# Filler products taken out, first products reordered and last copies split in a convolution-and-MLP kernel

## The chip, the cores and the metric

The kernel runs on one core of a Trainium2 chip. A core has five engines that run side by side and meet only through semaphores: TensorE for matrix products (PE in the profile; PEld is its weight load, which may overlap the product before), VectorE (DVE), ScalarE (ACT), GpSimd (POOL) and SyncE (SP), which here only issues DMAs. Products land in PSUM, which the kernel cuts into tiles of two banks (128 partitions x 1024 floats). The metric is the device time of one execution in microseconds (us). The median of three runs of the kernel before is 217.84 us (217.82 to 217.86).

## The reference

For a sequence of 2048 tokens and 512 channels the layer computes, in bfloat16 in and out:

```python
k_shift = sum over t of k_pad[:, t:t+S, :] * shift_k[:, ks-1-t]      # 4 taps
kv   = k_shift * v
kv_f = rfft2(pad(kv, S), axes=(1, 2))      # length 4096
kf_f = rfft2(pad(ssm_k, S), axes=(1, 2))
y    = irfft2(kv_f * kf_f)[:S] + kv * ssm_D
h    = x + layernorm(x) * y
h2   = h + relu(layernorm(h) @ w1) @ w2
```

The middle axis has length one, so the transform is a one-dimensional convolution of `kv` with `ssm_k` along the tokens, done by a Fourier transform of length 4096.

## The kernel before, in words

The transform is written as two stages of matrix products in each direction. "K" is the filter `ssm_k` and "X" is `kv`; their stage-1 results are the tiles BK and BX in SBUF.

Before the transform, `fill` (L153) multiplies a tile of zeros 22 times while the first data arrive. `to_rows` (L270) turns a 128 x 2048 array into rows: four steps `h` of eight TensorE transposes into a PSUM tile `pst`, each copied out in one piece, by ScalarE for h = 0 and 2 (L278) and by VectorE for h = 1 and 3 (L280). For K the target is `kfl`, for X it is `xfl`. `stage1` (L283) then runs for eight groups `gb` for each of K and X. A group takes two PSUM tiles, `pss[0]` and `pss[1]`, 32 small products (L293), and copies out. For K, VectorE adds a mask `dmask` to one half of each tile (L305) while ScalarE copies the other half (L308). For X, ScalarE copies the first tile (L266) and VectorE the second (L268); in X's group 3 ScalarE copies both. With `more=1`, which all of X's groups have, a group begins with one product of zeros into `pss[1]` (L288, recorded at L156).

`taps` (L332) computes 512 tokens by two channel blocks of the shifted `k` with eight products (L336), and VectorE multiplies the result by `v` in place (L330). K's groups 0 to 5 alternate with `taps`; the last two `taps` stand ahead of K's group 6. X's `to_rows` can only start after the last of these products with `v`. K's group 7 comes behind X's transposes, then X's eight groups, then four products of zeros (L394).

The product stage (L436) makes 16 groups of three units: `sums` for two frequencies (L427), and `pairs` (L418) twice. Each unit multiplies tables by BK into the left half of a PSUM tile and by BX into the right half; ScalarE copies the left half out (L409) and VectorE multiplies it by the right half, back into BX or BK (L433). The tables of `sums`, `smc`, are built by GpSimd (L381).

Inverse stage 1 (`inv1`, L518) makes 16 steps `b`. A step takes one PSUM tile, four groups of three products (one from BX at L523, two from BK at L526), and two copies out, one for each parity `rho`, into `ax[0]` (in BX's memory) and `ax[1]`. One letter for each copy says which engine does it: both on ScalarE, both on VectorE, and in the last step one each. Four products of zeros follow (L557), then inverse stage 2 (`inv2`, L604), which needs all of `ax`, and the MLP in four chunks (L616, L629).

What sets the order: the kernel is scheduled by hand, so each engine runs its instructions in the order of the program text. Up to the end of inverse stage 1 all PSUM tiles come from one pool of four buffers in rotation (L93), so a fifth tile waits until the first has been read. The framework adds the semaphore waits. Early on, GpSimd fills constants, scales the table `r2` (L228), builds `dmask` (L230, L237); VectorE reduces `r2` with `wrap13` (L220, called at L318) and derives small per-row constants (L311 to L315) ahead of K's `to_rows`.

Of the kernel before, what the change touches and what calls it, by code (L numbers as in the profile page):

```python
# [56 lines left out]
def kernel(  # L57
# [170 lines left out]
    nc.gpsimd.tensor_scalar(out=r2, in0=r2, scalar1=n2c[:], scalar2=2048.0, op0=ALU.mult, op1=ALU.add)  # L228
    dmask = early.tile([P, 2, 2, 16, 2, DC], BF16, name="dmask")
    nc.gpsimd.memset(dmask[:], 0.0)  # L230
    for dp in range(2):
        row = slice(64 * dp, 64 * dp + 1)
        for rp in range(2):
            for sp in range(2):
                src = draw[row, 256 * rp:256 * rp + 256].rearrange("p (r u s l d) -> p r u s l d", r=2, s=2, l=2, d=2)[:, :, :, sp, :, dp]
                for w in range(2):
                    nc.gpsimd.tensor_copy(out=dmask[row, rp, sp, :, w].rearrange("p u (r l) -> p r u l", l=2), in_=src)  # L237


    k1o = consts.tile([P, 1], F32, name="k1o")  # L240
# [29 lines left out]
    def to_rows(src, h, fl):  # L270

        pst = bank2("pst").rearrange("p b (i c) -> p (b i) c", i=4)
        srcw = src.bitcast(F32).rearrange("p c (a w) -> p (c a) w", w=32)
        for i in range(8):
            nc.tensor.transpose(out=pst[:, i, :], in_=srcw[:, :, 8 * h + i], identity=identw[:])  # L275
        o = fl.bitcast(I32)[:, :, 8 * h:8 * h + 8]
        if h % 2 == 0:
            nc.scalar.copy(out=o.bitcast(F32), in_=pst.rearrange("p i c -> p c i"))  # L278
        else:
            nc.vector.tensor_single_scalar(out=o, in_=pst.bitcast(I32).rearrange("p i c -> p c i"),  # L280
                                           scalar=0, op=ALU.bitwise_or)

    def stage1(fl, B, gb, dmul=None, xe="AD", more=0):  # L283

        j, sp = gb // 2, gb % 2
        pss = [bank2("ps1").rearrange("p b (a w r l x) -> p (b a) (w r) l x", a=2, w=2, r=2, l=2) for _ in range(2)]
        if more:
            fill(pss[1].rearrange("p u c l x -> p (u c l x)")[:, 0:512], more)  # L288
        for gi in range(8):
            g = 16 * j + 4 * (gi // 2) + 2 * sp + gi % 2  # L290
            for f, first in ((f1hi, True), (f1lo, False)):
                for rp, rows in enumerate(halves):
                    nc.tensor.matmul(out=pss[rp][:, gi // 2, :, gi % 2, :],  # L293
                                     lhsT=fl[rows, 2 * g:2 * g + 2, :].rearrange("p d n -> p (d n)"),
                                     rhs=f[rows].rearrange("p w r v h -> p (w r v h)"), start=first, stop=not first,
                                     tile_position=(64 * rp, 0), skip_group_check=True)
        o = [B.rearrange("p i (u w) (v s) x -> p i u w v s x", w=2, s=2)[:, :, 4 * j:4 * j + 4, :, :, sp, 4 * rp:4 * rp + 4]
             .rearrange("p i u w v x -> p i (u w) v x") for rp in range(2)]
        pv = [p.rearrange("p u (w r) l (v i) -> p i (u w) v (r l)", w=2, i=2) for p in pss]
        if dmul is None:  # L300
            for rp in range(2):
                copy(xe[rp], o[rp], pv[rp])
            return
        for rp in range(2):
            nc.vector.tensor_tensor(out=o[rp][:, 0], in0=pv[rp][:, 0],  # L305
                                    in1=dmul[:, rp, sp, 4 * j:4 * j + 4].rearrange("p u w x -> p (u w) x").unsqueeze(2)
                                    .to_broadcast([P, 8, 16, 4]), op=ALU.add)
            nc.scalar.copy(out=o[1 - rp][:, 1], in_=pv[1 - rp][:, 1])  # L308

    for t, sh, op in ((0, 2, ALU.logical_shift_right), (1, 3, ALU.bitwise_and)):  # L310
        nc.vector.tensor_single_scalar(out=pi4[:, t:t + 1], in_=pi4[:, t:t + 1], scalar=sh, op=op)  # L311
    nc.vector.tensor_scalar(out=k1o[:], in0=pi4[:, 0:1], scalar1=2.0, scalar2=1.0, op0=ALU.mult, op1=ALU.add)
    nc.vector.tensor_copy(out=rof[:], in_=pi4[:, 1:2])
    for t, v in ((esc, TURN / 8192), (ebi, -0.5 * TURN)):
        nc.vector.tensor_scalar(out=t[:], in0=rows4[:], scalar1=rof[:], scalar2=v, op0=ALU.is_equal, op1=ALU.mult)  # L315
    for h in range(4):
        to_rows(sk, h, kfl)
    wrap13(r2)  # L318
    big_sin(st[:, :, 0:64], tsn, 1)

    def more_sines(i):
# [3 lines left out]
        else:  # L325
            big_sin(st[:, half, 64:128], r2[:, half], 1)

    def product(c, h, src):
        vv = vT[:, 2 * h:2 * h + 2, CH * c:CH * c + CH]
        nc.vector.tensor_tensor(out=vv, in0=src, in1=vv, op=ALU.mult)  # L330
# [13 lines left out]
    for gb in range(7):  # L344
        if gb == 6:
            taps(3, 0)
            taps(3, 1)
            ec_sins(0, (2, 3))
        stage1(kfl, BK, gb, dmask)
        if gb < 4:  # L350
            more_sines(gb)
        if gb == 1:
            ec_turns(0)
        if gb == 3:
            ec_wrap(0)
        if gb in (4, 5):
            ec_sins(0, (gb - 4,))
        if gb < 6:
            taps(gb // 2, gb % 2)
# [52 lines left out]
    def pairs(k1):  # L412

        ps = bank2("u")
        for x, B in enumerate((BK, BX)):
            for i, t in ((0, st[:, k1, 64:192]), (1, st[:, k1, 0:128])):
                for dp, pq in enumerate(halves):
                    nc.tensor.matmul(out=ps[:, dp, 256 * x:256 * x + 256], lhsT=t[pq], rhs=cols(B, pq, k1, i),  # L418
                                     start=(i == 0), stop=(i == 1), tile_position=(64 * dp, 0), skip_group_check=True)
        return ps[:, :, 256:512], forms(ps[:, :, 0:256], "ktu"), BK[:, :, :, k1, :]  # L420

    def sums(k1):
        ps = bank2("us")
        for k in (k1, k1 + 1):
            for x, B in enumerate((BK, BX)):
                for i in range(2):
                    nc.tensor.matmul(out=ps[:, k % 2, 256 * x:256 * x + 256], lhsT=smc[:, k // 4 % 4, i, k % 4, :],  # L427
                                     rhs=cols(B, slice(0, P), k, i), start=(i == 0), stop=(i == 1), skip_group_check=True)
        return ps[:, :, 256:512], forms(ps[:, :, 0:256], "kts"), BX[:, 0, :, k1:k1 + 2, :].rearrange("p g k x -> p k g x")

    def times(unit):
        ps, kt, o = unit
        nc.vector.tensor_tensor(out=o, in0=ps.rearrange("p b (g x) -> p b g x", x=8),  # L433
                                in1=kt[:].rearrange("p b (g x) -> p b g x", x=8), op=ALU.mult)
# [82 lines left out]

    def inv1(b, eng):  # L518
        ps = bank2("psi").rearrange("p b (i d a n) -> p (b i) d a n", i=2, d=2, a=2)
        for i in range(4):  # L520
            g = 4 * b + i
            o = ps[:, i].rearrange("p d a n -> p (d a n)")
            nc.tensor.matmul(out=o, lhsT=BX[:, 0, g // 2, :, g % 2::2].rearrange("p c r -> p (c r)"), rhs=inv3[:].rearrange("p d a n -> p (d a n)"),  # L523
                             start=True, stop=False, skip_group_check=True)
            for dp in range(2):
                nc.tensor.matmul(out=o, lhsT=BK[:, dp, g // 2, :, g % 2::2].rearrange("p c r -> p (c r)"),  # L526
                                 rhs=inv12[:, 2 - 2 * dp:6 - 2 * dp, :].rearrange("p a n -> p (a n)"),
                                 start=False, stop=(dp == 1), skip_group_check=True)
        for rho in range(2):
            copy(eng[rho], ax[rho][:, :, :, 8 * b:8 * b + 8],  # L530
                 ps.rearrange("p i d a n -> p a n (i d)")[:, rho].rearrange("p (n m) c -> p n m c", m=2))

    lift(0)
    column_means((0,))
# [179 lines left out]
```

## Time and profile before

| | before |
|---|---|
| median of 3 runs | 217.84 us |
| the profiled execution | 217.85 us |
| its span in the trace | 215.9 us |
| PE busy | 204.9 us, 95% of the span |
| DVE busy | 142.0 us, 66% |
| ACT busy | 114.8 us, 53% |
| POOL busy | 61.5 us, 28% |

The difference between the profiled execution and its span, 1.95 us, lies around the recorded instructions. "Busy" of PE counts a product from its start to a modelled end, and counts products of zeros as well. In the rows of the timeline a line reads: start, duration, engine, line of the kernel, operation, tile written <- tile read, shape, count, and in brackets how long the engine had been idle and what ended that. The chain of waits follows the end of the execution back through whatever released each instruction; its rows read: start, duration, engine, tile, line.

### The profile page before, as it was taken

The numbers are of one execution on the slowest core, as the hardware profiler recorded it, in microseconds if no ns is written. First come the engines' busy times: TensorE is split into PE (matmuls) and PEld (weight loads), VectorE is DVE, ScalarE is ACT, GpSimd is POOL, SyncE is SP. The second block draws the span as 40 slices with busy tenths as digits, with TensorE's granted clock in tenths as the row PEclk, the third lists the DMA queues.
The fourth block names the chain that finished last, engine by engine and source line by source line (L and its number), as shares of the span: only waits on it lengthen the run. The fifth ranks groups of instructions, "written<-read, shape, count | busy, mean of one in ns | idle before, by whom it ended". The sixth has DMA issues, their size and how long they took to land.

```text
span 215.9 us, 4338 instructions
## 1 busy us (share of the span) xinstructions
PE 204.9 (95%) x1750; PEld 138.8 (64%) x1750; DVE 142.0 (66%) x240; ACT 114.8 (53%) x183; POOL 61.5 (28%) x116
## 2 busy tenths in 40 slices
PE   7879999999999999999999999999999999999990
PEld 2465555876888888889998964448444844444440
DVE  6998988768487887789673296799068833261121
ACT  6677786688667767735586029700980056026300
POOL 7497505993365500032001102620202020002000
PEclk9999999999999999999999999999999999999998
DMA  5999960000700000035503996977916615010011
GB/s 164 329 221 187 190 93 3 0 5 6 258 3 0 3 0 3 0 97 100 97 3 98 277 204 125 216 141 130 125 22 121 137 33 100 25 53 20 0 53 47
DMA packets 47687, 19.93 MB, mean 92 GB/s; under 512 B 42706, under 2 KB 46132, under 8 KB 47668
## 3 DMA queue, kind: packets, MB, share of 16 engines
q1 hardware_dynamic: 44144, 16.15, 38.0%
q10 hardware_dynamic: 3524, 3.51, 5.6%
q8 instruction: 14, 0.23, 0.4%
q14 instruction: 5, 0.04, 0.1%
HBM read 7.02 MB, written 2.10 MB: 42 GB/s over the span
## 4 chain that ended last, share of the span: by engine, by line
PE 80%; DVE 11%; ACT 4%; issue 1%; DMA 1%; DVEq 0%
PE ps2m L629 18%; PE ps1m L616 14%; PE u L418 9%; PE us L427 9%; PE psi L526 7%; PE pkv L336 7%; PE ps L293 6%; PE pz L604 5%; PE psi L523 4%; PE pst L275 2%; ACT BX L261 2%; DVE E L44 1%; ACT BX L266 1%; DVE st L473 1%; ACT M L618 1%
## 5 line engine op out<-in xcount | busy, mean ns | idle before, releaser
L618 ACT ACTIVATE M<-ps1m 128x512 bf16<-128x512 f32 (+1 forms) x44 | 25.0, 602 | 49.8 <-PE ps1m L616 27.2
L629 PE MATMUL ps2m<-M 128*128 128x512 bf16 (+1 forms) x176 | 38.7, 379 | 0.0
L629 PEld LDWEIGHTS <-M 128*128 128x128 bf16 (+1 forms) x176 | 17.1, 98 | 20.9 <-ACT M L618 0.4
L616 PEld LDWEIGHTS <-w 128*128 128x128 bf16 (+1 forms) x176 | 17.4, 100 | 20.4 <-issue 0.8
L381 POOL TENSOR_TENSOR smc<-st 64x256 fp32r<-64x256 f32 x32 | 22.7, 728 | 13.2 <-PE us L427 12.3
L632 DVE SCALAR_TENSOR_TENSOR M<-ps2m,rstd,M 128x512 bf16<-128x512 f32 x12 | 9.0, 748 | 24.7 <-PE ps2m L629 16.2
L526 PE MATMUL psi<-inv,BK 128*128 128x256 f32 x128 | 23.2, 283 | 0.2 <-DVE BK L433 0.2
L477 POOL TENSOR_SCALAR rstd<-mv 128x4 f32<-128x4 f32 x8 | 2.2, 276 | 69.5 <-DVE mv L475 69.5
L433 DVE TENSOR_TENSOR BK<-u,ktu 128x512 fp32r<-128x512 f32 x32 | 20.4, 680 | 0.0
L526 PEld LDWEIGHTS psi<-inv,BK 128*128 128x128 f32 x128 | 20.2, 195 | 0.4 <-DVE BK L433 0.4
L616 PE MATMUL ps1m<-xT,w 128*128 128x512 bf16 (+1 forms) x88 | 19.6, 379 | 0.2 <-ACT M L618 0.2
L616 PE MATMUL ps1m<-M,w 128*128 128x512 bf16 (+1 forms) x88 | 19.3, 379 | 0.0
L523 PE MATMUL psi<-inv,BX 128*128 128x256 f32 x64 | 18.3, 286 | 0.0
L409 ACT COPY ktu<-u 128x512 f32<-128x512 f32 x32 | 17.2, 588 | 1.6
L433 DVE TENSOR_TENSOR BX<-us,kts 128x512 fp32r<-128x512 f32 x16 | 11.1, 692 | 9.0 <-PE u L418 9.0
L427 PE MATMUL us<-BK,smc 128*128 128x256 f32 x64 | 14.7, 311 | 0.0
L409 ACT COPY kts<-us 128x512 f32<-128x512 f32 x16 | 9.4, 588 | 9.9 <-PE us L427 9.9
L418 PE MATMUL u<-BK,st 64*128 64x256 f32 x128 | 14.6, 306 | 0.0
L427 PE MATMUL us<-BX,smc 128*128 128x256 f32 x64 | 13.1, 285 | 0.2 <-DVE BX L268 0.2
L308 ACT CAST BK<-ps 128x512 fp32r<-128x512 f32 x16 | 9.4, 586 | 7.1 <-PE ps L293 5.2
L418 PE MATMUL u<-BX,st 64*128 64x256 f32 x128 | 13.0, 282 | 0.0
L523 PEld LDWEIGHTS psi<-inv,BX 128*128 128x128 f32 x64 | 12.5, 195 | 0.3 <-DVE BK L433 0.2
(124 smaller groups left out, 399.7 us busy)
## 6 DMA issues: line engine op xcount, KB each, us to landing
E<-in_A_ssm_k_dram SPq DMA_DIRECT2D x1, 2048.0 KB
out_dram<-M ACTq DMA_DIRECT2D x16, 128.0 KB
w<-in_B_w_dram SPq DMA_DIRECT2D x1, 1376.0 KB
M<-in_B_w_dram ACTq DMA_DIRECT2D x1, 1280.0 KB
M<-in_A_q_dram SPq DMA_DIRECT2D x8, 128.0 KB
xh<-in_A_q_dram SPq DMA_DIRECT2D x4, 128.0 KB
xr<-in_A_q_dram SPq DMA_DIRECT2D x4, 128.0 KB
M<-in_B_w_dram ACTq DMA_DIRECT2D x1, 96.0 KB
```

Source lines behind the costliest of these rows:

```text
L293: nc.tensor.matmul(out=pss[rp][:, gi // 2, :, gi % 2, :], lhsT=fl[rows, 2 * g:2 * g + 2, :].rearrange("p d n -> p (d n)"), rhs=f[rows].rea ...
L336: nc.tensor.matmul(out=ps[:, i, :], lhsT=wdiag[:, 2 * h + i, j, :], rhs=kT[c][:, 2 * h + i, 16 - j:CH + 16 - j], start=(j == 0), stop=(j = ...
L381: nc.gpsimd.tensor_tensor(out=smc[pq, c % 4, i, :, 64 * dp:64 * dp + 64], in0=st[pq, ks, 64:128].bitcast(F32), in1=st[pq, ks, 0:64].bitcas ...
L409: nc.scalar.copy(out=kt[:], in_=ps)
L418: nc.tensor.matmul(out=ps[:, dp, 256 * x:256 * x + 256], lhsT=t[pq], rhs=cols(B, pq, k1, i), start=(i == 0), stop=(i == 1), tile_position= ...
L427: nc.tensor.matmul(out=ps[:, k % 2, 256 * x:256 * x + 256], lhsT=smc[:, k // 4 % 4, i, k % 4, :], rhs=cols(B, slice(0, P), k, i), start=(i ...
L433: nc.vector.tensor_tensor(out=o, in0=ps.rearrange("p b (g x) -> p b g x", x=8), in1=kt[:].rearrange("p b (g x) -> p b g x", x=8), op=ALU.mult)
L523: nc.tensor.matmul(out=o, lhsT=BX[:, 0, g // 2, :, g % 2::2].rearrange("p c r -> p (c r)"), rhs=inv3[:].rearrange("p d a n -> p (d a n)"), ...
L526: nc.tensor.matmul(out=o, lhsT=BK[:, dp, g // 2, :, g % 2::2].rearrange("p c r -> p (c r)"), rhs=inv12[:, 2 - 2 * dp:6 - 2 * dp, :].rearra ...
L616: nc.tensor.matmul(out=ps1[:fsz, :].rearrange("p (i t) -> p i t", i=4), lhsT=w1[:, c, fc * P:fc * P + fsz], rhs=hT[sc][:, :, c, :], start= ...
L618: nc.scalar.activation(out=h1T[:fsz, fc, :], in_=ps1[:fsz, :], func=ACT.Relu)
L629: nc.tensor.matmul(out=ps2[:], lhsT=h1T[:ksz, fc, i * P:(i + 1) * P], rhs=w2[:ksz, fc, :], start=(fc == 0), stop=(fc == NFC - 1))
```

## The change

Nine edits, in the order of the program:

- GpSimd scales `r2` behind the construction of `dmask` and not ahead of it.
- In `to_rows`, step h = 3 is copied out in two pieces, the first bank by ScalarE and the second by VectorE. This holds for K and for X.
- VectorE does K's `to_rows` copies first, then `wrap13(r2)`, then the small constants.
- `taps(3, 1)` is multiplied by `v` in two instructions of 512 columns, one for each bank.
- X's groups of `stage1` have no product of zeros, and the four after them are gone.
- X's group 3 is shared by ScalarE and VectorE as the other groups are.
- In the product stage, `sums` puts K's four products ahead of X's four. In the first group (k1 = 0) K's products of all three units come ahead of X's products of all three. The copies out (`forms`) are written behind the products.
- In `inv1`, step 0 issues the BX product of i = 0 and of i = 2 first. In step 15 ScalarE copies both parities of the first bank (i = 0, 1) and VectorE both parities of the second (i = 2, 3), in pieces of 256 elements.
- Two products of zeros and not four follow inverse stage 1.

```diff
-    nc.gpsimd.tensor_scalar(out=r2, in0=r2, scalar1=n2c[:], scalar2=2048.0, op0=ALU.mult, op1=ALU.add)
     dmask = early.tile([P, 2, 2, 16, 2, DC], BF16, name="dmask")
...
+    nc.gpsimd.tensor_scalar(out=r2, in0=r2, scalar1=n2c[:], scalar2=2048.0, op0=ALU.mult, op1=ALU.add)
...
-        o = fl.bitcast(I32)[:, :, 8 * h:8 * h + 8]
-        if h % 2 == 0:
-            nc.scalar.copy(out=o.bitcast(F32), in_=pst.rearrange("p i c -> p c i"))
-        else:
-            nc.vector.tensor_single_scalar(out=o, in_=pst.bitcast(I32).rearrange("p i c -> p c i"),
-                                           scalar=0, op=ALU.bitwise_or)
+        o = fl.bitcast(I32)
+        for eng, i0, n in {0: (("A", 0, 8),), 1: (("D", 0, 8),), 2: (("A", 0, 8),), 3: (("A", 0, 4), ("D", 4, 4))}[h]:
+            oi, pi = o[:, :, 8 * h + i0:8 * h + i0 + n], pst[:, i0:i0 + n, :]
+            if eng == "A":
+                nc.scalar.copy(out=oi.bitcast(F32), in_=pi.rearrange("p i c -> p c i"))
+            else:
+                nc.vector.tensor_single_scalar(out=oi, in_=pi.bitcast(I32).rearrange("p i c -> p c i"),
+                                               scalar=0, op=ALU.bitwise_or)
...
-    def stage1(fl, B, gb, dmul=None, xe="AD", more=0):
+    def stage1(fl, B, gb, dmul=None):
...
-        if more:
-            fill(pss[1].rearrange("p u c l x -> p (u c l x)")[:, 0:512], more)
...
-                copy(xe[rp], o[rp], pv[rp])
+                copy("AD"[rp], o[rp], pv[rp])
...
+    for h in range(4):
+        to_rows(sk, h, kfl)
+    wrap13(r2)
     for t, sh, op in ((0, 2, ALU.logical_shift_right), (1, 3, ALU.bitwise_and)):
...
-    for h in range(4):
-        to_rows(sk, h, kfl)
-    wrap13(r2)
     big_sin(st[:, :, 0:64], tsn, 1)
...
-    def taps(c, h):
+    def taps(c, h, each=2):
...
-        product(c, h, ps)
+        for i in range(0, 2, each):
+            vv = vT[:, 2 * h + i:2 * h + i + each, CH * c:CH * c + CH]
+            nc.vector.tensor_tensor(out=vv, in0=ps[:, i:i + each, :], in1=vv, op=ALU.mult)
...
-            taps(3, 1)
+            taps(3, 1, 1)
...
-        stage1(xfl, BX, gb, xe="AA" if gb == 3 else "AD", more=1)
-    fill(bank2("psz")[:, 0, :], 4)
+        stage1(xfl, BX, gb)
...
     for k1 in range(0, 32, 2):
-        s2 = sums(k1)
-        for unit in [s2, pairs(k1), pairs(k1 + 1)]:
+        units = [sums(k1), pairs(k1), pairs(k1 + 1)]
+
+        for n, x in sorted(((n, x) for n in range(3) for x in range(2)), key=lambda nx: nx[::-1] if k1 == 0 else nx):
+            units[n][0](x)
+        for unit in units:
             times(unit)
...
+        for i, parts in (((0, (0,)), (2, (0,)), (0, (1, 2)), (1, (0, 1, 2)), (2, (1, 2)), (3, (0, 1, 2))) if b == 0 else
+                         [(i, (0, 1, 2)) for i in range(4)]):
+            of(i, parts)
+        for e, i0, n in ((eng, 0, 4),) if len(eng) == 1 else ((eng[0], 0, 2), (eng[1], 2, 2)):
+            for rho in range(2):
+                copy(e, ax[rho][:, :, :, 8 * b + 2 * i0:8 * b + 2 * i0 + 2 * n],
+                     ps[:, i0:i0 + n].rearrange("p i d a n -> p a n (i d)")[:, rho].rearrange("p (n m) c -> p n m c", m=2))
...
-        inv1(b, "AD" if b == 15 else "DD" if b in (3, 6, 8, 11, 14) else "AA")
+        inv1(b, "AD" if b == 15 else "D" if b in (3, 6, 8, 11, 14) else "A")
...
-    fill(bank2("psz")[:, 0, :], 4)
+    fill(bank2("psz")[:, 0, :], 2)
     M = bkp.tile([P, 32768], BF16, tag="K", name="M")
```

In the changed kernel `sums` and `pairs` return a function `do(x)` that issues the products of K (x = 0) or X (x = 1); `of(i, parts)` issues parts 0 (BX), 1 and 2 (BK) of group i of a step of `inv1`.

More of the change, by code (lines that the diff above doesn't have):

```diff
@@ L326, in more_sines @@
             big_sin(st[:, half, 64:128], r2[:, half], 1)
-    def product(c, h, src):
-        vv = vT[:, 2 * h:2 * h + 2, CH * c:CH * c + CH]
-        nc.vector.tensor_tensor(out=vv, in0=src, in1=vv, op=ALU.mult)
-    def taps(c, h):
+    def taps(c, h, each=2):
         ps = bank2("pkv")
@@ L414, in pairs, with do @@
         ps = bank2("u")
-        for x, B in enumerate((BK, BX)):
+        def do(x):
             for i, t in ((0, st[:, k1, 64:192]), (1, st[:, k1, 0:128])):
                 for dp, pq in enumerate(halves):
-                    nc.tensor.matmul(out=ps[:, dp, 256 * x:256 * x + 256], lhsT=t[pq], rhs=cols(B, pq, k1, i),
+                    nc.tensor.matmul(out=ps[:, dp, 256 * x:256 * x + 256], lhsT=t[pq], rhs=cols((BK, BX)[x], pq, k1, i),
                                      start=(i == 0), stop=(i == 1), tile_position=(64 * dp, 0), skip_group_check=True)
-        return ps[:, :, 256:512], forms(ps[:, :, 0:256], "ktu"), BK[:, :, :, k1, :]
+        return do, ps, "ktu", BK[:, :, :, k1, :]
     def sums(k1):
         ps = bank2("us")
-        for k in (k1, k1 + 1):
-            for x, B in enumerate((BK, BX)):
+        def do(x):
+            for k in (k1, k1 + 1):
                 for i in range(2):
                     nc.tensor.matmul(out=ps[:, k % 2, 256 * x:256 * x + 256], lhsT=smc[:, k // 4 % 4, i, k % 4, :],
-                                     rhs=cols(B, slice(0, P), k, i), start=(i == 0), stop=(i == 1), skip_group_check=True)
-        return ps[:, :, 256:512], forms(ps[:, :, 0:256], "kts"), BX[:, 0, :, k1:k1 + 2, :].rearrange("p g k x -> p k g x")
+                                     rhs=cols((BK, BX)[x], slice(0, P), k, i), start=(i == 0), stop=(i == 1), skip_group_check=True)
+        return do, ps, "kts", BX[:, 0, :, k1:k1 + 2, :].rearrange("p g k x -> p k g x")
     def times(unit):
-        ps, kt, o = unit
-        nc.vector.tensor_tensor(out=o, in0=ps.rearrange("p b (g x) -> p b g x", x=8),
+        do, ps, tag, o = unit
+        kt = forms(ps[:, :, 0:256], tag)
+        nc.vector.tensor_tensor(out=o, in0=ps[:, :, 256:512].rearrange("p b (g x) -> p b g x", x=8),
                                 in1=kt[:].rearrange("p b (g x) -> p b g x", x=8), op=ALU.mult)
     for k1 in range(0, 32, 2):
-        s2 = sums(k1)
-        for unit in [s2, pairs(k1), pairs(k1 + 1)]:
+        units = [sums(k1), pairs(k1), pairs(k1 + 1)]
+        for n, x in sorted(((n, x) for n in range(3) for x in range(2)), key=lambda nx: nx[::-1] if k1 == 0 else nx):
+            units[n][0](x)
+        for unit in units:
             times(unit)
@@ L519, in inv1, with of @@
         ps = bank2("psi").rearrange("p b (i d a n) -> p (b i) d a n", i=2, d=2, a=2)
-        for i in range(4):
+        def of(i, parts):
             g = 4 * b + i
             o = ps[:, i].rearrange("p d a n -> p (d a n)")
[L523 to L531, printed above, removed]
+            for part in parts:
+                src = BX[:, 0] if part == 0 else BK[:, part - 1]
+                rhs = inv3[:].rearrange("p d a n -> p (d a n)") if part == 0 else                     inv12[:, 4 - 2 * part:8 - 2 * part, :].rearrange("p a n -> p (a n)")
+                nc.tensor.matmul(out=o, lhsT=src[:, g // 2, :, g % 2::2].rearrange("p c r -> p (c r)"), rhs=rhs,
+                                 start=(part == 0), stop=(part == 2), skip_group_check=True)
+        for i, parts in (((0, (0,)), (2, (0,)), (0, (1, 2)), (1, (0, 1, 2)), (2, (1, 2)), (3, (0, 1, 2))) if b == 0 else
[5 more added lines that the diff above has]
+                     ps[:, i0:i0 + n].rearrange("p i d a n -> p a n (i d)")[:, rho].rearrange("p (n m) c -> p n m c", m=2))
     lift(0)
```

## The prediction

> **What bounds the kernel now.** I read the page's busy shares first: PE is busy for 204.9 of 215.9 us, so time is won only where PE is held up or does work nobody needs. The chain of waits shows where. Here it is from K's last group to the second product group (start, duration, engine, tile, line):
>
> ```profile
> 40.50 1.23 DVE xfl L280
> 41.73 0.61 DVE BK L305
> 42.36 0.59 ACT BK L308
> 42.99 0.38 PE ps L156
> 43.37 1.00 PE ps L293 x32
> 44.37 0.32 PE ps L156
> 44.69 1.00 PE ps L293 x32
> 45.69 0.32 PE ps L156
> 46.01 1.04 PE ps L293 x32
> 47.06 1.92 ACT BX L266 x2
> 49.02 1.07 PE ps L293 x32
> ...
> 51.74 1.04 PE ps L293 x32
> 52.80 1.24 DVE BX L268
> 54.04 0.14 issue
> 54.17 0.95 PE us L427 x6
> 55.13 1.18 PE u L418 x12
> 56.31 1.17 PE us L427 x8
> ```
>
> An X group costs PE 0.32 of zeros and 1.00 of products, 1.32, while VectorE's copy takes 1.23: PE sets the pace with the zeros in it, and waits once for ScalarE's two copies of group 3. Then PE stands behind the last copy of X, as only two K products were ahead of it.
>
> The timeline's rows for the start of K and for the end of inverse stage 1:
>
> ```profile
> 9.17 3.01 POOL L228 TENSOR_SCALAR G<-G,n2c 128x2048 int32<-128x2048 int32 x1 [3.17 <-DVE G L222]
> 10.74 1.47 DVE L315 TENSOR_SCALAR esc<-rows,rof 128x4 f32<-128x4 f32 x1
> 12.24 2.34 DVE L280 TENSOR_SCALAR E<-pst 128x1024 int32<-128x1024 int32 x2
> 14.51 1.21 DVE L220 TENSOR_SCALAR G<-G 128x2048 int32<-128x2048 int32 x1
> 15.89 1.38 DVE L305 TENSOR_TENSOR BK<-ps,dmask 128x512 fp32r<-128x512 f32 x2 [0.17 <-POOL dmask L237]
> ...
> 118.27 0.69 DVE L268 CAST ax<-psi 128x512 fp32r<-128x512 f32 x1 [0.77 <-ACT BX L266]
> ```
>
> The last row is the one to notice. In step 15 both engines read the same tile, and VectorE waited until ScalarE had finished.
>
> **Halves of a tile do not overlap.** Four edits share a tile between engines or cut a copy in two "by bank". The changed kernel as built carries these waits: in both `to_rows` and in step 15, ScalarE's piece waits for the last product of the whole tile and VectorE's piece waits for ScalarE's; the first half of the product of `taps(3, 1)` waits for the eighth of its eight products. Waits stand by tile, not by bank, as in the last row above. So I cost these edits in series, and they lose a little each.
>
> **Step by step, on PE's clock.** Prices of one copy: ScalarE 0.59 (512 elements) and 1.01 (1024); VectorE 0.69 and 1.23. The difference per element gives about 0.38 and 0.42 for 256. A copy right behind another of its engine starts about 0.1 before the end of the one ahead (two VectorE copies of 512 take 1.28, two of ScalarE 1.08).
>
> *K's start.* Before, `kfl` was complete at 14.58, as VectorE's first copy came late (12.24) behind `esc`, which took 1.47 where its twin `ebi` took 0.22, while GpSimd scaled `r2` until 12.18. Now VectorE's h = 1 copy is done at about 12.8, but h = 3 is in series: ScalarE from 13.36 (behind h = 2's copy, where its sine began at 13.34) to 13.95, VectorE 0.03 later for 0.69, to 14.67: 0.09 late. Then `wrap13` (1.21) and the constants (0.73 without the stall of `esc`) stand ahead of K's first adds, which start at about 16.4, not 15.89. ScalarE's copy of the same tile follows the first add: done at 17.7, not 17.20. PE's group 1 needs that buffer: it starts at 17.8, not 17.64. Take **+0.17**; at worst +0.5 (the whole delay of the adds), at best -0.5 (the halves of h = 3 overlap). GpSimd: `dmask` from 6.0 takes 0.56 + 4.04, `r2` 3.01 behind it, ready at 13.6, a microsecond before `wrap13` wants it; if `r2` were later still, the adds would be late by the excess. After group 1 VectorE needs 2.51 of each 2.84 us round, so the delay doesn't grow.
>
> *`taps(3, 1)`.* One product of 1.23 becomes two, 1.28 to 1.38 as for L305 x2. PE's transposes wait for it: **+0.10** (0.05 to 0.15).
>
> *X's rows.* ScalarE 0.59, 0.03, VectorE 0.69 in place of VectorE's 1.23: **+0.09**. So far PE is 0.36 late: X's group 0 starts at 42.14, not 41.78.
>
> *X's stage.* Without zeros PE offers a group in 1.00, so VectorE's copy (1.23, or 1.17 between starts as in 2.34 for two) sets the pace, and with four buffers a group may start when the copy of the group two before it ends. Following both: first copy 1.1 after PE's start, copies then every 1.17 to 1.23, eight of them. The last ends 10.74 after the start; before, 54.04 - 41.78 = 12.26. **-1.52**. Bounds: nothing lost between copies, 1.1 + 7 x 1.17 + 1.23 = 10.5, -1.74; the old pace of 1.32, 11.6, -0.69 (group 3's double copy alone and no product of zeros to speak of).
>
> *First product group.* Before, PE's second group began at 56.24, 2.20 after X's last copy. K's twelve products (half of 1.17 + 1.17, so 1.17) now fit ahead of that copy's end: two units' buffers are free earlier, the third's comes free with ScalarE's last X copy about 0.25 before VectorE's. Left is the other 1.17 and 0.09 to wake: 1.26. **-0.94**. If the third unit's K products came late, 0.29 less. In later groups `sums` has the same eight products, and VectorE (3 x 0.69) and ScalarE (3 x 0.59) fit beneath 2.34 or so of PE; costed at nothing on that cover.
>
> *Inverse stage 1.* In step 0 PE waited for the last BK (93.25). One more product of 0.12 goes ahead of that: **-0.12**. Step 15: ScalarE 0.38 + 0.28, 0.03, VectorE 0.42 + 0.33 make 1.44 against 0.59 + 0.03 + 0.70 = 1.32: **+0.11** (0 to 0.25). The two dropped products of zeros ran beneath this wait (ended at 118.5; PE went on at 119.11): nothing. The load of `w2` is issued behind ScalarE's copies, 19 us ahead of its first use.
>
> Behind this every DMA and wait is released by the end of inverse stage 1 or by later work, so the lead is kept to the end; `w1` (issued at 52.84, when `xfl` is read out) simply leaves earlier.
>
> Sum: 0.17 + 0.10 + 0.09 - 1.52 - 0.94 - 0.12 + 0.11 = -2.11. Against the profiled execution, 217.85 (the median is 217.84), that is 215.74, **215.7 us**.
>
> **Rivals.**
>
> *Slower: PE's clock drops in X's stage.* The page's granted clock is full throughout, but it doesn't show everything. The first products of zeros came 0.43 apart while it read 1.00, then 0.21 apart:
>
> ```profile
> 4.99 0.15 PEld L156 LDWEIGHTS <-zero 128*128 128x128 bf16 x1 [0.28 <-issue]
> 5.42 0.15 PEld L156 LDWEIGHTS <-zero 128*128 128x128 bf16 x1 [0.27 <-issue]
> 5.84 2.06 PEld L156 LDWEIGHTS <-zero 128*128 128x128 bf16 x10 [0.28 <-issue]
> ```
>
> So PE has a half-speed state. Without zeros it is busy for 1.00 of 1.2 us in X's stage. A group at half speed would take 2.0, about 0.85 over the pace; three such groups of eight eat the 2.11, and five give 220.0. Against it: PE idled for 1.44 us at 13.29, after transposes alone since 9.47, and the next 32 products took 1.07, near the 1.00 of later ones. The gaps here are 0.2.
>
> The Trainium skill speaks against the change: "TensorE: Matmul & The Clock Gate", section "A second HAM failure mode: psum-queue depth-cycling", says that a PE that idles briefly between groups while it cycles through PSUM banks can swing between half and full clock. By that rule alone X's groups would swing too; by the 1.44 us row they stay fast. No row of this trace shows such a swing.
>
> *The zeros were not what held X.* If pace stays 1.32, set by handing buffers over, term four shrinks to -0.69: -1.28, 216.6.
>
> *The split by bank works as meant.* If pieces overlapped in spite of the waits: `kfl` 0.63 earlier than now; `taps` half a product, 0.5 after the 0.10; X's rows 0.6; step 15 about 0.6. Some 2 us more, 213.5. The built waits speak against it.
>
> **How the numbers follow.** Main case 0.78, its own range 215.2 to 216.3 (0.17 up to 0.5 and the buffer's 0.29 one way, -1.74 and a free start the other). Zeros not the bound 0.10. Clock 0.08. Split works 0.04. The range 214.9 to 216.9 holds the first two with some slack and leaves out the other two. A change within 0.2%, 0.44 us, can't be told from none here. Faster: 0.78 + 0.09 + 0.04, 0.91; slower by more than that 0.07 of the clock case; 0.02 between.
>
> **What would show it.** After: no L156 rows from 40 to 52; X's VectorE copies back to back, 1.17 to 1.25 between starts, and 32 products still in 1.00; twelve K products ahead of the first BX product; the second product group at about 54.1. VectorE's piece in `to_rows` and in step 15 idle until ScalarE's piece ends. Group 1 of K no earlier than 17.6. Groups of X at 2.0, or a second product group after 55.5, would make the prediction wrong; overlapping pieces would make it too slow.

## The result, and the profile after

The changed kernel takes 215.93 us (median of 4 runs, 215.84 to 215.98), the kernel before 217.85 us in the same session. The ratio is 0.9911, with a 95% interval of 0.9894 to 0.9929: faster by 0.9%. The forecast was 215.7 us in a range of 214.9 to 216.9.

The profiled execution took 215.98 us, 1.87 less than before; its span is 214.18 us where it was 215.95, 1.77 less. The other 0.10 us lies outside the recorded instructions, and nothing here explains it.

These are rows of the timeline of the changed kernel (start, duration, engine, line, operation, tile written <- tile read, shape, count, and in brackets the engine's idle time and what ended it), from K's start to the end of inverse stage 1:

```profile
9.56 3.84 PE L276 MATMUL pst<-identw,E 128*128 128x128 f32 x32 [1.02 <-DMA E<-in_A_ssm_k_dram]
14.06 0.69 DVE L283 TENSOR_SCALAR E<-pst 128x512 int32<-128x512 int32 x1 [1.21 <-ACT E L281]
16.50 1.28 DVE L306 TENSOR_TENSOR BK<-ps,dmask 128x512 fp32r<-128x512 f32 x2
17.65 0.42 PE L294 MATMUL ps<-f_hi,E 64*128 64x128 bf16 x2
17.86 0.26 PE L294 MATMUL ps<-f_lo,E 64*128 64x128 bf16 x2
...
36.98 3.82 PE L276 MATMUL pst<-identw,E 128*128 128x128 f32 x32 [0.43 <-PE ps L294]
41.47 0.69 DVE L283 TENSOR_SCALAR xfl<-pst 128x512 int32<-128x512 int32 x1 [1.21 <-ACT xfl L281]
43.41 9.46 DVE L269 CAST BX<-ps 128x1024 fp32r<-128x1024 f32 x8
51.63 0.73 PE L427 MATMUL us<-BK,smc 128*128 128x256 f32 x4
52.28 0.90 PE L417 MATMUL u<-BK,st 64*128 64x256 f32 x8
53.12 0.74 PE L427 MATMUL us<-BX,smc 128*128 128x256 f32 x4
53.79 0.76 PE L417 MATMUL u<-BX,st 64*128 64x256 f32 x8
54.48 0.75 PE L427 MATMUL us<-BK,smc 128*128 128x256 f32 x4
...
115.77 0.37 ACT L267 CAST BX<-psi 128x256 fp32r<-128x256 f32 x1 [1.26 <-PE psi L531]
116.04 0.38 ACT L267 CAST ax<-psi 128x256 fp32r<-128x256 f32 x1
116.45 0.42 DVE L269 CAST BX<-psi 128x256 fp32r<-128x256 f32 x1 [0.83 <-ACT ax L267]
117.35 0.35 PE L613 MATMUL pz<-core,BX 128*128 128x256 f32 x1 [1.17 <-DVE ax L269]
```

Three things are to be seen. X's eight VectorE copies are one block of 9.46 us, 1.18 from one to the next, where before they came 1.32 apart: VectorE sets the pace of X's stage now. VectorE's piece in both `to_rows` and in step 15 starts only when ScalarE's piece of the same tile has ended ("<-ACT"), so the pieces stand in series. And the first product group has twelve K products ahead of the first X product, but the second group begins 1.61 after the last X copy (52.87), not 1.26 as I had it.

The same points of both traces, as differences of after to before:

| step of the prediction | predicted | measured | from which rows |
|---|---|---|---|
| K's start | +0.17 | +0.27 | VectorE's last product with `v` starts at 35.32, 35.59 |
| `taps(3, 1)` | +0.10 | +0.11 | X's transposes 36.60, 36.98 |
| X's rows | +0.09 | +0.06 | X's first product 41.78, 42.22 |
| X's stage | -1.52 | -1.61 | end of the last X copy 54.04, 52.87 |
| first product group | -0.94 | -0.59 | second group 56.24, 54.48 |
| step 0 of `inv1` | -0.12 | -0.12 | end of inverse stage 1 117.46, 115.58 |
| step 15 | +0.11 | +0.12 | first pz 119.11, 117.35 |
| sum | -2.11 | -1.76 | VectorE's last start 210.78, 209.04: -1.74 |

### The profile page after: what moved, and what is told of

Read it like the earlier page. It is cut to its first block, busy times and chain, and to the rows that moved or that the text cites. A ratio compares the mean times of both kernels' runs of the same rounds, so it can differ in the third digit from the quotient of the medians.

```text
span 214.2 us, 4311 instructions
## 1 busy us (share of the span) xinstructions
PE 202.7 (95%) x1736; PEld 138.1 (64%) x1736; DVE 140.8 (66%) x243; ACT 114.9 (54%) x185; POOL 61.6 (29%) x116
## 5 line engine op out<-in xcount | busy, mean ns | idle before, releaser
L477 DVE BATCH_NORM_STATS2 st<-M 128x6 f32<-128x512 bf16 x20 | 12.3, 678 | 0.0
L599 DVE TENSOR_TENSOR qT<-pz,qT 128x2048 bf16<-128x2048 f32 x2 | 4.6, 2291 | 11.3 <-DMA qT<-M 7.3
```

The costliest lines, as they stand in the source:

```text
L477: nc.vector.bn_stats(out=st[:, i, :], in_=src[:, i, :])
```

## The experiments

My theory of X's stage and of the first group had to be parted from each other, the waits by tile from the rival that pieces overlap, and the two terms that came out wrong had to be explained. Each kernel is the changed one with one edit, unless another is named. The kernel before took 217.85 to 217.94 us beside them.

### The products of zeros

```diff
-        stage1(xfl, BX, gb)
+        stage1(xfl, BX, gb, more=1)     # one product of zeros ahead of a group, as before
```

> The changed kernel with one product of zeros again at the head of each of X's eight groups (the four behind them stay out, group 3 stays shared). Theory (the zeros set X's pace): 32 products and the zeros make 1.32 per group against VectorE's 1.18 between copies, so X's last copy ends about 1.1 later (54.0 after the span's start, not 52.87), and the time is 217.0 against 215.93. Rival 1 (the pace of X is set by handing buffers over, not by PE): same pace, 215.9. Rival 2 (without zeros PE ran slower somewhere and the zeros protected it): 215.5 or less, with shorter products elsewhere.

217.20 us, ratio 0.9971 (0.9941 to 1.0001). Rows of its timeline in X's stage:

```profile
46.01 0.39 PE L156 MATMUL ps<-zero 128*128 128x512 bf16 x1
46.11 1.01 ACT L267 CAST BX<-ps 128x1024 fp32r<-128x1024 f32 x1 [0.31 <-PE ps L296]
47.33 0.39 PE L156 MATMUL ps<-zero 128*128 128x512 bf16 x1
```

The groups are 47.33 - 46.01 = 1.32 apart again, although ScalarE takes one tile of every group as in the changed kernel. The second product group begins at 55.59, 1.11 later than without zeros, and the time is 1.27 more. So the zeros were the bound of X's stage; that rival is out. Of the 1.9 us won they are the greater part. From X's first product to the end of its last copy the stage takes 11.81 us here (42.17 to 53.98), 10.65 in the changed kernel and 12.26 before. So 1.16 of its 1.61 are the zeros; the other 0.45 is what is left for sharing group 3's copies, which no run put back alone.

### K's products ahead

```diff
-        for n, x in sorted(..., key=lambda nx: nx[::-1] if k1 == 0 else nx):
+        for n, x in sorted(..., key=lambda nx: nx):
```

> The changed kernel with the first product group in the order of all others (sums with K then X, then each pairs with K then X), zeros still out. If the prediction's term for K's products ahead were right (0.94) this would cost 0.9: 216.9. The changed kernel's profile says otherwise: its second group begins 1.61 behind X's last copy, not 1.26. If each change between the full-array products of sums and the half-array products of pairs costs about 0.2, as the rows of later groups suggest (4 products of 0.117 take 0.58 to 0.67 where a change precedes them), the old order starts its second group 0.1 + 0.67 + 1.16 = 1.93 behind the copy: 0.3 later, 216.25.

216.33 us, ratio 0.9930 (0.9917 to 0.9942). Its timeline at the first product group:

```profile
53.06 0.73 PE L427 MATMUL us<-BX,smc 128*128 128x256 f32 x4 [0.67 <-DVE BX L269]
53.72 0.51 PE L417 MATMUL u<-BK,st 64*128 64x256 f32 x4
...
54.90 0.75 PE L427 MATMUL us<-BK,smc 128*128 128x256 f32 x4
```

Here PE stands idle for 0.67 us until X's last copy is done (52.92) and has the pairs of K still to do. The second group begins at 54.90, 1.98 behind that copy; in the changed kernel it begins 1.61 behind it, in the kernel before 2.20. So K's `pairs` ahead of X's products are worth 0.37 us in the trace and 0.40 in the time. The other 0.22 of the 0.59 is the order within `sums`. Before, only two of its four K products stood ahead of the wait, and six products followed it, from 54.17 to 55.06; here four follow it, from 53.06 to 53.72. No run put that order back alone. The four products of zeros that stood ahead of the first group did not hold it: after them PE still idled until VectorE's last copy was done.

Why only 0.37? The eight K products that left X's half are worth 0.48: with them it takes 1.84 (53.06 to 54.90), without them 1.36 (53.12 to 54.48). But X's half now starts 0.25 behind the last copy and not 0.14, as the K products end only at 53.12; that takes 0.11 back. And 1.36 is more than half a group, 1.17. The rows of the changed kernel say why. Products of `sums` start 0.12 apart, so four are worth 0.48; yet X's four take from 53.12 to 53.79, 0.67, and the eight of a later group take 1.16. In both cases about 0.2 us stands beside the products. It is the price of a change of PE from full-array products (`sums`, 128 rows) to half-array ones (`pairs`, 64 rows) or back. A later group has two such changes. The first group, with K ahead of X, has four, two of them in X's half. To test that, all groups in that order:

```diff
-        for n, x in sorted(..., key=lambda nx: nx[::-1] if k1 == 0 else nx):
+        for n, x in sorted(..., key=lambda nx: nx[::-1]):
```

> The changed kernel with every product group in the order of the first: K's products of sums and both pairs, then X's. The same products, tables and copies; a group then enters each kind of product (full-array sums, half-array pairs) twice and not once. Theory (each entry costs 0.22 of PE: 8 products at 0.117 take 1.16 in a later group): 15 groups x 2 x 0.22 = 6.6 more, 222.5, less if other waits are filled by it. Rival (the first group took 1.36 for its X half only because buffers came late): no price of its own, 216 to 217.

229.03 us, ratio 1.0532 (1.0495 to 1.0569), more than was expected. One group in its timeline:

```profile
67.26 0.75 PE L427 MATMUL us<-BK,smc 128*128 128x256 f32 x4
68.06 0.30 PEld L417 LDWEIGHTS u<-BK,st 64*128 64x128 f32 x4 [0.27 <-DVE BX L434]
68.66 0.30 PEld L417 LDWEIGHTS u<-BK,st 64*128 64x128 f32 x4 [0.30 <-DVE BK L434]
...
70.47 0.75 PE L427 MATMUL us<-BK,smc 128*128 128x256 f32 x4
```

From `us` to `us` of the next group it is 3.21 us, 0.88 over the 2.33 of the usual order. Two more changes make 0.4, which is what was expected; the other 0.45 or so are waits for PSUM buffers that VectorE had yet to read ("<-DVE"), and those I had missed.

If a change costs 0.2, groups in alternating order (sums, pairs, pairs, then pairs, pairs, sums) save one change per group:

```diff
-        units = [sums(k1), pairs(k1), pairs(k1 + 1)]
+        units = [sums(k1), pairs(k1), pairs(k1 + 1)] if k1 % 4 == 0 else [pairs(k1), pairs(k1 + 1), sums(k1)]
```

> The changed kernel with sums, pairs, pairs in even product groups and pairs, pairs, sums in odd ones, so that sums meets sums and pairs meets pairs at the border of two groups. Theory of the entries: 15 entries of 0.22 fewer, 3.3 less, down to where VectorE's three products (3 x 0.60 to 0.69) set the pace, so 2.1 per group and not 2.33: 212.6, plus up to 0.4 since the last unit is now one whose result all of inverse stage 1 waits for. Rival (entries cost nothing): 215.9 to 216.3.

217.15 us, ratio 0.9969 (0.9948 to 0.9991): a miss by 4.5 us. Its waits between 56 and 90 us (engine, tile and line that waited <- who ended it: total us, times, longest):

```profile
ACT ktu L407 <- DVE BK L434: 5.6, 8, 0.7
DVE BX L434 <- PE u L417: 4.4, 7, 0.6
PEld u L417 <- DVE BX L434: 3.2, 7, 0.5
```

The changes are saved (the sixteen products of two neighbouring `sums` run with none between them, from 65.48 to 67.62: 2.14, again 0.12 each and 0.2 beside them), but two groups take 4.80 us, not the 4.66 of before. VectorE's product for `sums` writes into BX, waits there until PE's `pairs` have read it, and frees its PSUM tile so late that PE waits in turn. The other phase, pairs first in the first group, fares the same:

> As the alternating kernel, but even groups begin with pairs and odd ones with sums, so that the last group ends with pairs as before and X's stage 1, whose products are half-array too, meets pairs. Theory of the entries: one entry fewer at the start and no late sums at the end, but the first group's sums takes the buffer that ScalarE's last copy of X frees: between 212.3 and 212.7. Rival as there: 215.9.

216.97 us, ratio 0.9960 (0.9945 to 0.9975). Sixteen products of `sums` take 2.14 here too. So the changes were saved both times, but the cover under which the copies had lain was gone.

### Halves in one tile, and in two

First the shared copies undone: h = 3 of `to_rows`, `taps(3, 1)` and step 15 as before the change.

```diff
-        ... 3: (("A", 0, 4), ("D", 4, 4))}[h]
+        ... 3: (("D", 0, 8),)}[h]
-            taps(3, 1, 1)
+            taps(3, 1)
-        for e, i0, n in ((eng, 0, 4),) if len(eng) == 1 else ((eng[0], 0, 2), (eng[1], 2, 2)):
+        for i0, n in ((0, 4),):          # and engine rho of the pair copies parity rho
```

> The changed kernel with all three shared copies undone: h = 3 of both to_rows whole on VectorE, the product of taps(3, 1) in one instruction, step 15 with one parity on ScalarE and the other on VectorE over the whole tile. Theory (two engines' pieces of one tile run one after the other, so each split only adds): K's start 0.1 to 0.15 earlier, taps 0.05, X's rows 0.08, step 15 0.12: 215.6. Rival (the splits gain by sharing): slower than 215.93 by 0.5 or more, 216.4 up.

215.69 us, ratio 0.9900 (0.9886 to 0.9913): faster than the changed kernel by 0.24. X's copies start at 43.19 and not 43.41, and the first pz at 117.04 and not 117.35. The three edits lose a little, as was costed.

Then the two halves of step 15 in two PSUM tiles, so that no piece has to wait for the other's tile:

```diff
-        ps = bank2("psi").rearrange("p b (i d a n) -> p (b i) d a n", i=2, d=2, a=2)
+        if len(eng) == 1:
+            tiles = [bank2("psi").rearrange("p b (i d a n) -> p (b i) d a n", i=2, d=2, a=2)]
+        else:
+            tiles = [bank2("psi")[:, 0, :].rearrange("p (i d a n) -> p i d a n", i=2, d=2, a=2) for _ in range(2)]
```

> The changed kernel with one difference: in step 15 of inverse stage 1 each half has its own PSUM tile. If the wait by tile was what kept the two engines in a row there, ScalarE starts as soon as the products of i = 0 and 1 are done and VectorE as soon as those of i = 2 and 3 are: the first pz starts 0.7 to 0.75 us earlier after psz's last product than in the changed kernel, and the time is 215.2 to 215.3. Rival: the two engines would be held by reading neighbouring banks, or the last product and its copy set the end anyway: 215.9.

215.40 us, ratio 0.9871 (0.9843 to 0.9899). Its timeline at step 15:

```profile
115.02 0.37 ACT L267 CAST BX<-psi 128x256 fp32r<-128x256 f32 x1 [0.54 <-PE psi L535]
115.29 0.38 ACT L267 CAST ax<-psi 128x256 fp32r<-128x256 f32 x1
115.73 0.42 DVE L269 CAST BX<-psi 128x256 fp32r<-128x256 f32 x1
116.08 0.42 DVE L269 CAST ax<-psi 128x256 fp32r<-128x256 f32 x1
116.64 0.36 PE L617 MATMUL pz<-core,BX 128*128 128x256 f32 x1 [0.71 <-DVE ax L269]
```

ScalarE starts 0.75 earlier, VectorE directly after its own products, and the first pz 0.71 earlier (0.04 of it was there before step 15). So the wait by tile had held both engines. ScalarE ends (115.67) before VectorE begins (115.73), so this run does not tell whether the two can read PSUM at the same time; X's rows in the next one do. The gain in time, 0.53 by the medians and 0.62 by the profiled executions, is a little under that.

The same for all three places, with two tiles for h = 3 of `to_rows` and for `taps(3, 1)` too:

```diff
-        pst = bank2("pst").rearrange("p b (i c) -> p (b i) c", i=4)
+        if h == 3:
+            pst = [bank2("pst")[:, 0, :].rearrange("p (i c) -> p i c", i=4) for _ in range(2)]
...
-        ps = bank2("pkv")
+        ps = [bank2("pkv")[:, 0, :] for _ in range(2)] if each == 1 else bank2("pkv")
```

> The changed kernel with each half in a PSUM tile of its own (two buffers of the pool, one bank used in each) for h = 3 of both to_rows, for taps(3, 1) and for step 15, so that the pieces no longer wait for each other; the copies are the same instructions. Theory (the waits stand by tile, and they are what the split lost): pieces run side by side; kfl complete near 14.1 and not 14.75, K's second group 0.55 earlier, transposes of X another 0.35, X's rows 0.6, step 15 0.6: about 213.9. Rival (the two engines can't read side by side, or extra buffers taken from the pool of four cost as much): 215.6 to 216.

214.58 us, ratio 0.9850 (0.9836 to 0.9863): 1.35 under the changed kernel, but 0.7 over what was expected. Its timeline at K's rows, X's rows, the start of X's stage and the second product group:

```profile
13.56 0.69 DVE L288 TENSOR_SCALAR E<-pst 128x512 int32<-128x512 int32 x1 [0.81 <-PE pst L280]
...
35.98 3.87 PE L280 MATMUL pst<-identw,E 128*128 128x128 f32 x32
...
38.98 1.50 ACT L286 COPY xfl<-pst 128x1024 f32<-128x1024 f32 x2 [0.68 <-PE pst L280]
39.88 0.69 DVE L288 TENSOR_SCALAR xfl<-pst 128x512 int32<-128x512 int32 x1 [0.58 <-PE pst L280]
41.10 1.35 DVE L311 TENSOR_TENSOR BK<-ps,dmask 128x512 fp32r<-128x512 f32 x2 [0.52 <-PE ps L299]
42.36 2.45 DVE L269 CAST BX<-ps 128x1024 fp32r<-128x1024 f32 x2
...
54.69 0.51 PE L422 MATMUL u<-BK,st 64*128 64x256 f32 x4
```

VectorE's pieces wait for PE now ("<-PE pst"), not for ScalarE. In X's rows ScalarE's piece, the second of its two copies, ends at 40.48, and VectorE's runs beside it from 39.88 to 40.57; both take as long as in the changed kernel. X's transposes start 1.00 earlier than in the changed kernel. `xfl` is complete at 40.57, 4.59 after them, where it took 5.18. But this second gain of 0.59 stops at the next bound: K's group 7 is still to be added and copied out, VectorE ends that at 42.45, and its first copy of X starts 6.38 after the transposes, where it had started 6.43 after them.

### The small constants

```diff
+    ...                                  # pi4, k1o, rof, esc, ebi: VectorE's small constants
     for h in range(4):
         to_rows(sk, h, kfl)
     wrap13(r2)
-    ...
```

> The changed kernel, with VectorE's small constants (0.73 us without a stall) ahead of K's row copies again; GpSimd keeps its new order. My step put all of the late start of K's group 1 (17.83 in the changed kernel, 17.57 before) down to the adds, which start at 16.50 where they started at 15.89. If that is so, the adds start near 15.9, group 1 near 17.6 or as soon as TensorE has finished the products of taps ahead of it (17.7), and the time is 215.93 less 0.15 to 0.25: about 215.75. Rival: the constants meet GpSimd's work again, as in the kernel before, where one of them took 1.47 instead of 0.23. Then VectorE's first row copy is late by over 1 us, the sine waits for it, and the time is 216.2 or more.

215.79 us, ratio 0.9889 (0.9859 to 0.9919). Its timeline at K's start:

```profile
9.41 3.84 PE L276 MATMUL pst<-identw,E 128*128 128x128 f32 x32 [1.75 <-DMA E<-in_A_ssm_k_dram]
11.25 0.27 DVE L316 TENSOR_SCALAR esc<-rows,rof 128x4 f32<-128x4 f32 x1
15.77 1.34 DVE L306 TENSOR_TENSOR BK<-ps,dmask 128x512 fp32r<-128x512 f32 x2
17.51 0.23 PE L294 MATMUL ps<-f_hi,E 64*128 64x128 bf16 x2
17.57 0.22 PE L294 MATMUL ps<-f_lo,E 64*128 64x128 bf16 x2
```

`esc` takes 0.27 here and 1.47 before the change; what GpSimd ran beside it differs, the small copies of `dmask` here and one operation over 128 x 2048 there, which ended at 12.18, as `esc` did at 12.21. The adds start at 15.77, and group 1's products follow each other from 17.51 with no gap, where in the changed kernel the first began at 17.65 and the second was held until 17.86, 0.15 longer than the usual 0.06. The spans of the two traces differ by 0.30: half is this gap, half the load of `ssm_k`, whose transposes began at 9.41 and not at 9.56. The 0.14 us between the medians fits the gap, but the kernel before differs by 0.09 between the same two sessions, so the rows carry this more than the time does.

On the kernel with two tiles:

> The variant with a PSUM tile for each half (214.58), with the small constants ahead of K's row copies as well. By the same reasoning group 1 of K, which started at 17.23 there, could start near 17.1, and the time would be about 214.4, down to 214.3. Rival: TensorE's own products of taps set the start of group 1 there already, and nothing is won: 214.6; or the constants stall beside GpSimd's work: 215 or more.

214.59 us, with 214.41 to 214.69 in four runs and 215.66 and 215.84 in two; ratio 0.9849 (0.9815 to 0.9883). Nothing beyond the 214.58 of the kernel that it builds on can be told from this. The profiled execution is one of the two, and its stretches show why (columns: span and its length, then busy time of PE, PEld, DVE, ACT, POOL with counts, the granted clock, DMA share and GB/s):

```profile
9.57:15.10 5.53, 5.44 (x32) 5.25 (x32) 3.26 (x9) 2.25 (x3) 4.08 (x7) 0.69 1.15 228
```

K's 32 transposes took 5.44 us at a mean granted clock of 0.69. In the changed kernel they took 3.84 at 1.00. They had come 2.06 us after the last product of zeros, in the other kernels with these products 0.5 to 1.8 after it.

### What the zeros at the start are good for

The clock rival had PE at half speed in X's stage. To see when PE is at half speed at all, the 22 products of zeros at the very start were left out.

```diff
-    fill(bank2("psz")[:, 0, :], 22)
```

> The changed kernel without the 22 products of zeros at the very start. If PE needs steady work to reach its full speed and nothing else gives it that in time, X's and K's first products run at half speed (32 products of stage 1 in 2 and not 1.0) until some 4 to 5 us of work are done: 1.5 to 4 later, 217.5 to 220. Rival (the early half speed is only a matter of time since the start, and would be over by 9.5 anyway): 215.9. It tells how far the fear of a slower PE in X's stage was a fear of something that this kernel can show at all.

218.1 us (217.14 to 218.79), ratio 1.0005 (0.9982 to 1.0027): 2.2 us slower than the changed kernel. The profiled execution was the fastest, 217.14; what the slower ones lost beyond it, no trace shows. PE's timeline at its start, and two stretches of the transposes (columns as above):

```profile
9.42 5.07 PE L275 MATMUL pst<-identw,E 128*128 128x128 f32 x32 [9.42 <-DMA E<-in_A_ssm_k_dram]
15.91 0.23 PE L293 MATMUL ps<-f_hi,E 64*128 64x128 bf16 x2 [1.42 <-DVE E L282]
15.97 0.22 PE L293 MATMUL ps<-f_lo,E 64*128 64x128 bf16 x2
```

```profile
9.42:11.00 1.58, 1.58 (x8) 1.58 (x9) 1.38 (x2) 0.00 (x0) 1.58 (x3) 1.00 1.06 233
12.50:14.50 2.00, 1.99 (x18) 1.80 (x17) 1.23 (x1) 0.88 (x1) 1.26 (x1) 1.00 1.10 194
```

From idle, the transposes take 5.07 instead of 3.84, which is about what this execution lost against 215.98. They start 0.21 apart until 12.02 and 0.11 apart from 12.20 on; the granted clock reads 1.00 in both stretches, so the half speed has to be read from the pace. After them and 1.42 us of idling the products are 0.06 apart, at full pace. So the half-speed state exists, it ended while PE did nothing but transposes, and a gap of 1.4 us did not bring it back. It is not a matter of time since the start: the products of zeros in the kernel before were at full pace from 5.84. X's stage, with gaps of 0.2, shows products 0.06 apart in every group.

### The best version

The price of a change suggests the first group in the order K sums, K pairs, K pairs, X pairs, X pairs, X sums, on the kernel with two tiles:

```diff
-        for n, x in sorted(..., key=lambda nx: nx[::-1] if k1 == 0 else nx):
+        for n, x in sorted(..., key=lambda nx: (nx[1], (nx[0] or 3) if nx[1] else nx[0]) if k1 == 0 else nx):
...
-        for unit in units:
+        for unit in units[1:] + units[:1] if k1 == 0 else units:
```

> The variant with a PSUM tile for each half (214.58), with the first product group in the order K sums, K pairs, K pairs, X pairs, X pairs, X sums. That has two entries between full-array and half-array products fewer (X's pairs follow K's pairs, the next group's sums follow X's sums). If an entry costs 0.2 us, as the groups showed, the second product group begins 0.4 earlier and the time is about 214.2. Rival: the unit copied out last now stands behind two others, its buffers or BX come late for the next group as in the alternating orders, and nothing is won or a little lost: 214.5 to 214.9.

214.04 us (213.97 to 214.16), ratio 0.9809 (0.9779 to 0.9839): 1.9 under the changed kernel, 0.54 under the kernel with two tiles alone. Its timeline at the first group:

```profile
51.24 0.96 PE L422 MATMUL u<-BK,st 64*128 64x256 f32 x8
52.03 0.67 PE L422 MATMUL u<-BX,st 64*128 64x256 f32 x8
52.63 0.76 PE L432 MATMUL us<-BX,smc 128*128 128x256 f32 x4
53.22 0.64 PE L432 MATMUL us<-BK,smc 128*128 128x256 f32 x4
...
54.28 0.51 PE L422 MATMUL u<-BK,st 64*128 64x256 f32 x4
```

X's four products of `sums` and the next group's eight run as twelve with no change among them, 54.28 - 52.63 = 1.65, once more 0.12 each and 0.2 beside them. The second group's `pairs` begin at 54.28; with two changes more, in the kernel with two tiles alone, they began at 54.69. So two changes cost 0.41 (the two profiled executions differ by 0.45). One group at the end of a row, with X's copies all done, has room for what sixteen alternating groups had no room for.

## Why the prediction was right, and which terms were off

**The mechanism held.** The zeros set X's pace, and without them VectorE's copies do: -1.52 predicted, -1.61 measured, and 1.27 us of the time come back with them alone. Of the 1.61, sharing group 3 accounts for about 0.45. The bounds, -1.74 and -0.69, held it.

**Halves of a tile in series.** Predicted from the row of step 15 before and from the built waits, shown three times: by the rows after ("<-ACT"), by undoing the splits (-0.24), and by giving step 15's halves two tiles (-0.53), all three places (-1.35). The rival that pieces of one tile overlap was refuted. The two-tile form, in which they do overlap, comes to 214.58 where the rival had said 213.5: 0.6 of that distance is X's rows, whose gain K's group 7 swallows.

**The clock** did not drop in X's stage. The Trainium skill's warning that brief idling between groups swings PE's clock ("TensorE: Matmul & The Clock Gate", section "A second HAM failure mode: psum-queue depth-cycling") was weighed against the 1.44 us gap of the trace, and no run here shows such a swing at gaps of 0.2.

**The term that was mis-sized** is "First product group. -0.94": it measured -0.59. The step that failed is "Left is the other 1.17 and 0.09 to wake: 1.26", where 1.61 was measured. I split a later group in two halves, but a later group has two changes between full-array and half-array products, and K first makes four of them, two in each half. X's half is therefore 53.12 to 54.48, 1.36, not 1.17. The other 0.16 is the start of X's half, 0.25 after the last copy and not 0.09. Part of this was named: the third unit's K products came late, as its buffer comes free with ScalarE's last copy (end 52.62), and the twelve K products end at 53.12. The measured 0.59 also contains 0.22 from the order within `sums`, which the step did not tell apart. A row that I had shown could have told that something stands beside the products: the chain of before has eight products of `sums` in 1.17, 0.146 each, while I costed a product of inverse stage 1, which has the same shape, at 0.12.

**K's start** was put at +0.17 by late adds. The gap that the adds made in group 1 is 0.15, and with their delay undone the gap is gone. Of the rest of the +0.27, 0.09 is the load of `ssm_k`: the transposes began at 9.56 in one trace and at 9.47 in the other, and I had no term for how loads differ from one execution to the next.

**`taps`, X's rows, step 0 and step 15** came within 0.03 of their sums. GpSimd's `r2` was ready at 13.82, costed as 13.6, still ahead of `wrap13` at 14.67. That came out by luck: the copies of `dmask` took 5.16 and not 4.04, and scaling `r2` took 1.99 and not 3.01.

The sum missed the trace by 0.35. The time missed by 0.24 in the profiled execution and by 0.19 in the median, since 0.10 us outside the span went the good way, which is no merit of the forecast.

## What to carry to other kernels

Products of zeros that keep an engine warm cost time in the one stage where that engine sets the pace, as far as the pace of the next engine: taking 0.32 us of zeros out of each group of X won 0.14 a group, from 1.32 to 1.18, where VectorE's copies set the pace. Look for them there, and test the fear of a slow clock by the longest gap that the trace shows without harm. Two engines that are to share a copy out of PSUM need two tiles here, since the waits stand by tile: the split in one tile lost 0.24 us here, in two tiles it won 1.1. A new order of products is priced with every change between full-array and half-array products (about 0.2 us each here) and with the copies that the old order covered.

## What the runs showed of the hardware that I had not expected

- A change between products over 128 rows and over 64 rows costs about 0.2 us of PE in either direction: 4, 8, 12 and 16 products of `sums` in a row take 0.67, 1.16, 1.65 and 2.14 us, 0.12 for each product and about 0.2 beside them, and leaving out two changes won 0.41.
- PE's half-speed state ended while PE did transposes alone (from idle, 32 of them in 5.07 us, 0.21 apart at first and 0.11 after 12.2; 3.84 otherwise). The Trainium skill says that the full clock doesn't engage for transposes in PE's transpose mode ("TensorE: Matmul & The Clock Gate", section "Part 4: PE-mode transpose"). The fp32 transposes here stand in the trace as products, and no row tells whether that mode was on; for them the pace was full from 12.2 on.
- In the one profiled execution in which the transposes came 2.06 us after the products of zeros, they started 0.11 apart up to 10.89, 0.21 apart from 11.06 to 14.26 and 0.11 apart again behind that, 0.69 of the full clock on the mean. After 1.83 us (the alternating groups) they ran at full speed throughout, 3.84. Whether the length of the gap or its place in time decided was not tried.
